# Groups of one batch, and a unit without attention that computes v on GpSimd, in a fused attention and two-MoE kernel

## The chip, the cores and the metric

The kernel runs on one core of one Trainium2 chip. The metric is the device time of one execution in microseconds (us); lower is better. The engines that matter are PE (TensorE, matrix multiplies), DVE (VectorE), ACT (ScalarE), POOL (GpSimd) and the DMA engines, which are fed from the queues of SP (SyncE) and POOL.

## What is computed

```python
# attention, batch by batch: 8 batches, 3072 tokens, 256 wide, keys of 64
scores = z @ z.T / 3072
out    = (relu(scores) ** 2) @ v
x      = u * out                                    # 24576 tokens x 256

# first MoE: a token with x @ w_skip > 0 goes to one of 8 experts (256 -> 1024 -> 256)
e      = argmax(x @ w_gate)
x[tok] += gate[tok] * (relu(x[tok] @ w1[e]) @ w2[e])

# second MoE: one dense rational layer (256 -> 2048 -> 256)
h = x @ w_in
P = a0 + a1*h + a2*h**2 + a3*h**3
Q = 1 + |b0|*|h| + |b1|*h**2
out = (P / (Q + 1e-6)) @ w_out
```

All of it is float32. Every large product is made of three passes of a split operand (high and low part), which is why there are pairs of tiles such as ah and al, mgh and mgl.

## The kernel before

**Work items.** Attention is cut into 1152 ticks (8 batches, 12 rows of 256 queries, 12 steps of 256 keys). A tick is 16 matmuls of 256 columns on PE (4 for the scores, L661 and L662; 12 for the product with v, L684), two or three ACT passes (L665, L668, L409) and one DVE subtraction (L676). After every 12 ticks a row of queries is routed: a chain of small steps over PE, ACT, DVE and POOL ends in indirect writes of the rows to a DRAM buffer xs, sorted by expert.

The MoE work is cut into 1024 units of 24 (or 18) matmuls on PE. 256 of them belong to the first MoE (kinds "m" and "n": ReLU on ACT, L1249, and one subtraction on DVE, L1252). 768 belong to the second (kinds "x" and "y"). A second-MoE unit evaluates the rational layer on a 128x512 tile h in PSUM:

- ACT: abs, u = |h| (L1257); p1 (L1258); ln (L1272) and ex (L1273), which turn the denominator q into its reciprocal u.
- q0 = b1\*u + b0 (POOL or DVE L1264, or ACT L1262) and q1 = q0\*u (L405, POOL or DVE).
- DVE: p2 (L1270), p3 (L1271), gh (L1274, the high part of the result, tile mgh), v = (q + c)\*gh (L1275), w (L1277), and gl (L405, POOL or DVE, the low part, tile mgl).

gh and gl feed the second product (L1095). h sits in one of five PSUM banks of ring "b" from the first matmul of the unit until w.

**Groups.** The batches are cut into groups of 1, 2, 2, 2 and 1. A group's attention is done, its rows are sorted by expert, its first-MoE units run (8 experts, 4 chunks of weights, and as many halves as the group has batches), and then its second-MoE units. In a group of two batches one chunk of first-MoE weights (tile W, 1 MB, loaded at L993 from the copy wsc1) serves two units, with matmuls of 512 columns (mm_l1w, L1077); in a group of one it serves one unit with matmuls of 256 columns (mm_l1, L1066). Attention ticks of the following groups are mixed among the units: kind "x" is a second-MoE unit that runs beside ticks, kind "y" one that runs after the last tick. The last group's first-MoE units are kind "n"; they use the attention's V buffers for weights (tile Wv) and run among "y" units. Between the last tick and the last group lie 56 "y" units of the group before (number POST) and the 32 "n" units; we call this stretch the bridge.

**Order.** The program's order is not that of the loops. Each step is given a due time (a place of its unit or tick on a line of PE time, plus an offset from LAG, plus a correction from the table PAR). The class Flow then lays the steps on the engines one by one with costs such as "D.602" (0.602 us on DVE) and ring sizes from RINGS, and each engine runs its own list in that order. W has a ring of 8 buffers, mu and mq of 3, mp of 2, mr (rows of a tile) of 4. SP's queue is in order too: a W load that waits for a free buffer holds up what stands behind it.

## Time and profile before

| | us |
|---|---|
| median of 3 runs | 5582.74 (5581.83 to 5587.68) |
| the profiled execution | 5577.05 |
| its span (first to last instruction) | 5575.3 |

| stretch of the profiled execution, us | length | what runs in it (counts from the loops) |
|---|---|---|
| 0 to 366 | 366 | attention alone, 168 ticks |
| 366 to 511 | 145 | group 0, first MoE: 32 m, and 12 ticks |
| 511 to 1301 | 790 | group 0, second MoE: 80 x with 276 ticks |
| 1301 to 1520 | 219 | group 1, first MoE: 64 m with 12 ticks |
| 1520 to 2663 | 1143 | group 1, second MoE: 192 x with 288 ticks |
| 2663 to 2882 | 219 | group 2, first MoE: 64 m with 12 ticks |
| 2882 to 3980 | 1098 | group 2, second MoE: 192 x with 264 ticks |
| 3980 to 4200 | 220 | group 3, first MoE: 64 m with 12 ticks |
| 4200 to 4895 | 695 | group 3, second MoE: 152 x with 108 ticks |
| 4895 to 5192 | 297 | bridge: 56 y and 32 n |
| 5192 to 5575 | 383 | group 4, second MoE: 96 y |

The limits of the stretches are the first ACT steps of their kind in the trace (abs of the second MoE, ReLU of the first), so the last steps of a unit spill over into the next stretch. Busy time of PE is modelled and counts overlapped matmuls; what PE does not fill is idle for certain, what it fills may still hold short waits.

### The profile page before, as it was taken

What the parts mean: (1) busy time and instruction counts of PE and PEld (TensorE: products, weight loads), DVE (VectorE), ACT (ScalarE), POOL (GpSimd) and SP (SyncE); (2) the same over time, 40 slices, a digit from 0 to 9 for tenths busy, and PEclk for the clock granted to TensorE, in tenths of its full rate; (3) what the DMA queues carried; (4) which work ended last, traced back from release to release, by engine and by line L of the source; (5) the groups of instructions that cost most, each with busy time, mean ns of one, the idle gap of its engine ahead of it and who ended that gap; (6) DMA issues with size and microseconds to landing.
All of it is one profiled execution on the core that took longest, in us unless ns stands there. A gap on an engine that the chain in (4) does not pass through costs nothing.

```text
span 5575.3 us, 107018 instructions
## 1 busy us (share of the span) xinstructions
PE 5362.4 (96%) x39525; PEld 5027.9 (90%) x39525; DVE 4533.8 (81%) x7470; ACT 4202.2 (75%) x7663; POOL 3090.5 (55%) x4422
## 2 busy tenths in 40 slices
PE   9989999999999999999999999999999999999887
PEld 8989999999899999999899989999988888888666
DVE  6765777774498999899459999999638999998998
ACT  8866888885388888888448888888627888855776
POOL 3433445443256655665235566556526667765887
PEclk9999999999999999999999999999999999999999
DMA  4375111114510110112541010011351000044000
GB/s 136 115 273 218 64 51 42 34 53 176 176 60 32 45 40 31 31 41 76 178 154 36 32 50 27 29 32 48 132 207 63 24 25 20 25 157 140 16 16 17
DMA packets 205545, 435.31 MB, mean 78 GB/s; under 512 B 30094, under 2 KB 129017, under 8 KB 181458
## 3 DMA queue, kind: packets, MB, share of 16 engines
q1 hardware_dynamic: 177746, 360.66, 19.1%
q0 software_dynamic: 27264, 67.71, 3.5%
q8 instruction: 313, 5.13, 0.4%
q14 instruction: 222, 1.82, 0.1%
HBM read 308.56 MB, written 153.22 MB: 83 GB/s over the span
## 4 chain that ended last, share of the span: by engine, by line
PE 70%; DVE 13%; ACT 6%; DMA 4%; issue 4%; POOL 3%; SPq 0%; DVEq 0%; ACTq 0%; POOLq 0%
PE accA L684 24%; PE h L1077 17%; PE accM L1095 16%; PE S L661 4%; PE S L662 4%; DVE mq L1275 3%; DVE mgh L1274 3%; DMA mr<-xs 2%; DVE h L1271 2%; DVE mq L1277 2%; DVE mp L1270 1%; PE lp L773 1%; PE mt L1130 1%; ACT mp L1258 1%; ACT mu L1272 1%
## 5 line engine op out<-in xcount | busy, mean ns | idle before, releaser
L1077 PE MATMUL h<-mx,W 128*128 128x512 f32 x5760 | 1540.7, 400 | 64.1 <-DVE mq L1277 58.9
L684 PE MATMUL accA<-V,ah 128*128 128x256 f32 x9216 | 1270.0, 280 | 13.1 <-ACT ah L409 8.3
L405 POOL TENSOR_TENSOR mgl<-mq,mu 128x512 fp32r<-128x512 f32 x655 | 892.1, 1363 | 692.9 <-DVE mq L1277 395.8
L1077 PEld LDWEIGHTS h<-mx,W 128*128 128x128 f32 x5760 | 1013.5, 190 | 250.6 <-DVE mq L1277 75.3
L684 PEld LDWEIGHTS accA<-V,ah 128*128 128x128 f32 x9216 | 1164.4, 189 | 31.5 <-ACT ah L409 14.5
L1095 PE MATMUL accM<-W,mgh 128*128 128x256 f32 x7680 | 1054.5, 280 | 10.6 <-DVE mgh L1274 6.6
L1095 PEld LDWEIGHTS accM<-W,mgh 128*128 128x128 f32 x7680 | 979.6, 189 | 32.3 <-DVE mgh L1274 8.9
L676 DVE TENSOR_TENSOR al<-S,ah 128x512 fp32r<-128x512 f32 x1152 | 786.3, 683 | 168.4 <-ACT ah L409 143.9
L665 ACT ACTIVATE S<-S 128x512 f32<-128x512 f32 x1152 | 677.9, 588 | 119.2 <-PE S L662 109.5
L684 PE MATMUL accA<-V,al 128*128 128x256 f32 x4608 | 729.7, 281 | 5.9 <-DVE al L676 5.7
L1264 POOL TENSOR_SCALAR mq<-mu,coef 128x512 f32<-128x512 f32 x554 | 458.0, 827 | 473.1 <-ACT mu L1257 467.6
L668 ACT ACTIVATE S<-S 128x512 f32<-128x512 f32 x1152 | 676.0, 587 | 21.8
L1270 DVE TENSOR_TENSOR mp<-mp,h 128x512 f32<-128x512 f32 x768 | 522.3, 680 | 187.0 <-ACT mp L1258 178.1
L1257 ACT ACTIVATE mu<-h 128x512 f32<-128x512 f32 x768 | 458.0, 596 | 271.0 <-PE h L1077 212.2
L409 ACT ACTIVATE ah<-S 128x512 fp32r<-128x512 f32 x996 | 594.9, 598 | 63.3 <-PE accA L684 41.7
L1095 PE MATMUL accM<-W,mgl 128*128 128x256 f32 x3840 | 615.1, 282 | 27.9 <-POOL mgl L405 27.3
L1274 DVE SCALAR_TENSOR_TENSOR mgh<-h,coef,mu 128x512 fp32r<-128x512 f32 x768 | 571.3, 744 | 80.2 <-ACT mu L1273 64.9
L684 PEld LDWEIGHTS accA<-V,al 128*128 128x128 f32 x4608 | 621.4, 189 | 13.5 <-DVE al L676 8.2
L1275 DVE SCALAR_TENSOR_TENSOR mq<-mq,mgh 128x512 f32<-128x512 f32 x768 | 617.4, 805 | 15.7 <-DVE mgh L1274 0.5
L1272 ACT ACTIVATE mu<-mq 128x512 f32<-128x512 f32 x768 | 483.3, 629 | 179.1 <-POOL mq L405 138.6
L1258 ACT ACTIVATE mp<-h,coef 128x512 f32<-128x512 f32 x768 | 595.5, 775 | 23.3 <-DVE h L1271 18.8
L1095 PEld LDWEIGHTS accM<-W,mgl 128*128 128x128 f32 x3840 | 537.3, 189 | 63.4 <-POOL mgl L405 39.7
(157 smaller groups left out, 8466.9 us busy)
## 6 DMA issues: line engine op xcount, KB each, us to landing
W<-wsc SPq DMA_DIRECT2D x96, 1024.0 KB
wsc<-W SPq DMA_DIRECT2D x32, 1024.0 KB
...
```

Of the source, the lines that this page charges most:

```text
L405: (nc.vector if e == "D" else nc.gpsimd).tensor_tensor(*a, **k)
L409: act(out, in_, AF.Copy)
L665: act(st["s"], st["s"], AF.Relu, scale=1.0 / S)
L668: act(st["s"], st["s"], AF.Square)
L676: ttt(st["lo"], st["s"], st["hi"].bitcast(F32), op=ALU.subtract)
L684: mm(accs[b, ic][:, it * TT : (it + 1) * TT], lhsT=a[:, jj * TT + it * P : jj * TT + (it + 1) * P], rhs=VV[b, jp][:, vi, jj * D : (jj + 1) ...
L1077: mm(h, lhsT=lw, rhs=rw, start=(k == 0 and i == 0), stop=(k == NK - 1 and i == 2), skip_group_check=True)
L1095: mm(accs_[it // 2][:, it % 2 * TT : (it % 2 + 1) * TT], lhsT=(gh, gl)[part][:, it * P : (it + 1) * P], rhs=w[i][:, 512 + ff * D : 512 + ( ...
L1258: pt("p1", "A.664", ["l1b"], lambda: act(buf("mp"), s["h"], AF.Identity, scale=a3, bias=a2), ["mp"])
L1270: pt("p2", "D.602", ["p1", "abs"], lambda: ttt(s["p"], s["p"], s["h"], op=ALU.mult))
L1274: pt("gh", "D.663", ["ex", "p3"], lambda: stt(buf("mgh", F32R), s["h"], a0, s["u"], op0=ALU.add, op1=ALU.mult), ["mgh"])
L1275: pt("v", "D.602s", ["gh"], lambda: stt(s["q"], s["q"], CQ, s["gh"].bitcast(F32), op0=ALU.add, op1=ALU.mult))
```

## The change

Three things change in the source, and with them the order of nearly all instructions:

- GROUPS becomes eight groups of one batch. All 256 first-MoE units now use one chunk of weights each, with matmuls of 256 columns. POST goes from 56 to 40 and MROW from 8 to 16 (12 ticks are spread over the first 16 units of a first-MoE stretch).
- "y" units compute differently. A new ACT step qc (L1281) adds the constant to q. v becomes a plain product on POOL (L1285) in place of the DVE step L1275. w writes into h (L1286), and gl (L1287) is always on DVE and reads h. q1 is always on POOL. mu uses the attention's T1 buffers (6) and mq the wr buffers (4) in place of 3 and 3. h is held until gl, not w. In the last group every sixth unit takes its h from the accumulator bank accA.
- The tables PAR, SLIP, AHEAD, LAG of "y" and the planned PE costs get new numbers, and two 64-byte spacers (ahead of T4 and V) are gone.

| after: stretch | what runs in it (counts from the loops) |
|---|---|
| attention alone; group 0, first MoE | 168 ticks; 32 m and 12 ticks |
| group 0, second MoE | 80 x with 132 ticks |
| groups 1 to 6, first MoE, each | 32 m with 12 ticks |
| groups 1, 2, 3, second MoE, each | 96 x with 144 ticks |
| groups 4, 5, second MoE, each | 96 x with 132 ticks |
| group 6, second MoE | 72 x with 72 ticks |
| bridge | 40 y and 32 n |
| group 7, second MoE | 96 y |

```diff
-GROUPS = [1, 2, 2, 2, 1]
+GROUPS = [1, 1, 1, 1, 1, 1, 1, 1]
...
-SLIP = {"P": 8.95, "A": 0.25, "D": 24.11, "G": 5.02, "Q": 9.0}
-LEAD, TAIL, POST, CARRY, MROW = 24, 8, 56, 1, 8
-PE_TICK, PE_UNIT = 1.92, 2.87
+SLIP = {"P": 8.1, "A": 0.25, "D": 32.01, "G": 33.99, "Q": 9.0}
+LEAD, TAIL, POST, CARRY, MROW = 24, 8, 40, 1, 16
+PE_TICK, PE_UNIT = 1.87, 2.8
...
+        home = {"mgh": ghb, "mgl": glb}
+        if kd == "y":
+            home.update(mu="T1", mq="wr")
...
-        hu = ("b", ("u", t))
+        hb = "accA" if kd == "y" and m.g == NG - 1 and (t - len(munits)) % 6 == 0 else "b"
+        hu = (hb, ("u", t))
...
-            pt("q1", "D.602s|G1.245t", ["q0"], lambda e: tt_on(e, s["q"], s["q"], s["u"], op=ALU.mult))
+            pt("q1", "G1.245t" if kd == "y" else "D.602s|G1.245t", ["q0"], lambda e="G": tt_on(e, s["q"], s["q"], s["u"], op=ALU.mult))
...
+            if kd == "y":
+
+                pt("qc", "A.52", ["q1"], lambda: act(s["q"], s["q"], AF.Identity, bias=CQ))
+                pt("ln", "A.52", ["qc"], lambda: act(s["u"], s["q"], AF.Ln))
+                pt("ex", "A.52", ["ln"], lambda: act(s["u"], s["u"], AF.Exp, scale=-1.0))
+                pt("gh", "D.663", ["ex", "p3"], lambda: stt(buf("mgh", F32R), s["h"], a0, s["u"], op0=ALU.add, op1=ALU.mult), ["mgh"])
+                pt("v", "G1.245t", ["gh"], lambda: pool_tt(s["q"], s["q"], s["gh"].bitcast(F32), op=ALU.mult))
+                pt("w", "D.663", ["v"], lambda: stt(s["h"], s["h"], a0, s["q"], op0=ALU.add, op1=ALU.subtract), (), ["mq"])
+                pt("gl", "D.602", ["w"], lambda: ttt(buf("mgl", F32R), s["h"], s["u"], op=ALU.mult), ["mgl"], ["mu"], [hu])
```

The order moves in these places. In the names, the number after h, mp, mq, mu, mgh and mgl is the unit; the last group of the kernel holds units 928 to 1023. DVE in the middle of the last group, before:

```order
L1270 TENSOR_TENSOR mp994_72646<-mp994_72646,h994_72582 128x512
L1277 SCALAR_TENSOR_TENSOR mq993_72629<-h993_72535,coef_103,mq993_72629 128x512
L1271 SCALAR_TENSOR_TENSOR h994_72582<-mp994_72646,coef_103,h994_72582 128x512
L1274 SCALAR_TENSOR_TENSOR mgh994_72720<-h994_72582,coef_103,mu994_72667 128x512
L1270 TENSOR_TENSOR mp995_72683<-mp995_72683,h995_72596 128x512
L1275 SCALAR_TENSOR_TENSOR mq994_72677<-mq994_72677,mgh994_72720 128x512
```

and after:

```order
L1286 SCALAR_TENSOR_TENSOR h994_74135<-h994_74135,coef_109,mq994_74195 128x512
L1278 SCALAR_TENSOR_TENSOR h996_74212<-mp996_74285,coef_109,h996_74212 128x512
L1287 TENSOR_TENSOR mgl994_74341<-h994_74135,mu994_74179 128x512
L1286 SCALAR_TENSOR_TENSOR h995_74174<-h995_74174,coef_109,mq995_74238 128x512
L1284 SCALAR_TENSOR_TENSOR mgh996_74361<-h996_74212,coef_109,mu996_74264 128x512
L1287 TENSOR_TENSOR mgl995_74364<-h995_74174,mu995_74216 128x512
L1277 TENSOR_TENSOR mp997_74314<-mp997_74314,h997_74231 128x512
```

DVE has five steps a unit in both. L1275 (v), which read the two SBUF tiles mq and mgh, is gone, and gl (L1287), which reads h, has come. POOL at the same place, before:

```order
L1264 TENSOR_SCALAR mq994_72677<-mu994_72667,coef_103 128x512
L405 TENSOR_TENSOR mq994_72677<-mq994_72677,mu994_72667 128x512
L405 TENSOR_TENSOR mgl992_72703<-mq992_72616,mu992_72602 128x512
L405 TENSOR_TENSOR mgl993_72712<-mq993_72629,mu993_72618 128x512
L1264 TENSOR_SCALAR mq995_72728<-mu995_72718,coef_103 128x512
```

and after:

```order
L1271 TENSOR_SCALAR mq996_74287<-mu996_74264,coef_109 128x512
L405 TENSOR_TENSOR mq996_74287<-mq996_74287,mu996_74264 128x512
L1285 TENSOR_TENSOR mq994_74195<-mq994_74195,mgh994_74298 128x512
L1285 TENSOR_TENSOR mq995_74238<-mq995_74238,mgh995_74308 128x512
L405 TENSOR_TENSOR mq997_74328<-mq997_74328,mu997_74296 128x512
L1271 TENSOR_SCALAR mq998_74351<-mu998_74338,coef_109 128x512
```

POOL's v (L1285) stands where its gl (L405 into mgl) stood. In the last 96 units POOL has 70 q0, 96 q1 and 96 gl before, and 73 q0, 96 q1 and 96 v after; ACT has 26 q0 before, and 23 q0 and 96 qc after. SP's queue in a first-MoE stretch of group 1 before (W is a chunk of weights, mr the rows of a tile):

```order
L1119 DMA mr17_0_20491<-xs1_73 128x516
L993 DMA W61_20525<-wsc1_70 128x2048
L1119 DMA mr17_1_20569<-xs1_73 128x516
L993 DMA W62_20583<-wsc1_70 128x2048
L993 DMA W63_20629<-wsc1_70 128x2048
L993 DMA W64_20705<-wsc1_70 128x2048
L1119 DMA mr18_0_20723<-xs1_73 128x516
```

and of group 2 after:

```order
L1119 DMA mr32_0_25131<-xs2_75 128x516
L993 DMA W98_25173<-wsc1_70 128x2048
L993 DMA W99_25224<-wsc1_70 128x2048
L993 DMA W100_25257<-wsc1_70 128x2048
L993 DMA W101_25308<-wsc1_70 128x2048
L763 DMA x2_3_78<-xs39_24278 128x2x256
L1119 DMA mr33_0_25337<-xs2_75 128x516
```

Four W loads lie between the rows of two tiles in both, but before they serve eight units, after four.

## Rows read from the trace of the kernel before

**Rows 1.** The page, busy time and share of PE and its span.
```profile
span 5575.3 us, 107018 instructions
...
PE 5362.4 (96%) x39525; PEld 5027.9 (90%) x39525; DVE 4533.8 (81%) x7470; ACT 4202.2 (75%) x7663; POOL 3090.5 (55%) x4422
```

**Rows 2.** Windows by stretch: limits, length, each engine's busy us (instructions), clock, DMA.
```profile
366.00:511.00 145.00, 128.06 (x1038) 125.03 (x1037) 76.98 (x133) 74.21 (x135) 39.73 (x73) 0.98 0.86 321
511.00:1301.00 790.00, 785.87 (x6266) 761.22 (x6264) 601.35 (x1049) 667.48 (x1287) 375.25 (x743) 1.00 0.17 55
1301.00:1520.00 219.00, 212.82 (x1448) 194.24 (x1447) 78.55 (x139) 70.20 (x127) 50.12 (x98) 1.00 0.54 191
1520.00:2663.00 1143.00, 1134.85 (x8549) 1074.10 (x8548) 1045.83 (x1736) 976.70 (x1792) 683.93 (x1000) 1.00 0.14 44
2882.00:3980.00 1098.00, 1086.97 (x8136) 1030.44 (x8135) 1018.66 (x1684) 945.78 (x1723) 672.35 (x940) 1.00 0.13 43
...
4200.00:4895.00 695.00, 662.40 (x4609) 608.10 (x4608) 669.88 (x1053) 574.27 (x1012) 502.10 (x553) 0.99 0.10 32
4895.00:5192.00 297.00, 274.08 (x1890) 249.61 (x1889) 265.80 (x384) 174.54 (x290) 186.59 (x190) 0.98 0.39 131
5192.00:5575.00 383.00, 301.79 (x1778) 250.77 (x1778) 359.79 (x500) 271.40 (x433) 325.11 (x265) 0.97 0.05 18
```

**Rows 3.** The same, abs alone (L1257): its count is the units' count.
```profile
1520.00:2663.00 1143.00, 114.53 (x192) 1.00 0.14 44
...
4200.00:4895.00 695.00, 90.65 (x152) 0.99 0.10 32
4895.00:5192.00 297.00, 33.45 (x56) 0.98 0.39 131
5192.00:5575.00 383.00, 56.98 (x96) 0.97 0.05 18
```

**Rows 4.** The same, the first ReLU of a tick alone (L665).
```profile
511.00:1301.00 790.00, 161.74 (x276) 1.00 0.17 55
...
4200.00:4895.00 695.00, 62.25 (x106) 0.99 0.10 32
```

**Rows 5.** DVE groups, 5200 to 5500: line, tiles, count | busy us, mean ns | idle before.
```profile
L1275 DVE SCALAR_TENSOR_TENSOR mq<-mq,mgh 128x512 f32<-128x512 f32 x78 | 80.3, 1029 | 3.2
L1277 DVE SCALAR_TENSOR_TENSOR mq<-h,coef,mq 128x512 f32<-128x512 f32 x79 | 58.4, 740 | 0.0
L1274 DVE SCALAR_TENSOR_TENSOR mgh<-h,coef,mu 128x512 fp32r<-128x512 f32 x78 | 58.3, 748 | 5.2 <-ACT mu L1273 1.0
L1271 DVE SCALAR_TENSOR_TENSOR h<-mp,coef,h 128x512 f32<-128x512 f32 x78 | 58.1, 745 | 0.7
L1270 DVE TENSOR_TENSOR mp<-mp,h 128x512 f32<-128x512 f32 x78 | 52.6, 675 | 1.3 <-ACT mp L1258 1.3
L1139 DVE TENSOR_TENSOR mx<-mt,mx 128x512 fp32r<-128x512 f32 x10 | 6.8, 682 | 0.0
```

**Rows 6.** DVE groups, 2000 to 2600: v beside attention.
```profile
L1275 DVE SCALAR_TENSOR_TENSOR mq<-mq,mgh 128x512 f32<-128x512 f32 x101 | 76.2, 754 | 1.7
```

**Rows 7.** POOL and ACT groups, 5200 to 5500.
```profile
L405 POOL TENSOR_TENSOR mgl<-mq,mu 128x512 fp32r<-128x512 f32 x79 | 114.7, 1452 | 6.3 <-DVE mq L1277 6.3
L405 POOL TENSOR_TENSOR mq<-mq,mu 128x512 f32<-128x512 f32 x78 | 106.1, 1370 | 4.1
...
L1272 ACT ACTIVATE mu<-mq 128x512 f32<-128x512 f32 x78 | 48.8, 626 | 43.2 <-POOL mq L405 43.2
L1264 POOL TENSOR_SCALAR mq<-mu,coef 128x512 f32<-128x512 f32 x59 | 47.4, 803 | 26.7 <-ACT mu L1257 26.7
```

**Rows 8.** Waits, 5200 to 5500: who for whom, us in total, times, longest.
```profile
PE h L1077 <- DVE mq L1277: 35.2, 45, 2.1
```

**Rows 9.** First-MoE matmuls of the last group (L1066): duration, first and last start.
```profile
L1066 PE MATMUL h<-mx,Wv x384: 274/283/387, 4931.8 to 5127.7; 128*128 128x256 f32 x192
```

**Rows 10.** PE group of the tile transposes, 1380 to 1520.
```profile
L1130 PE MATMUL mt<-ident_r,mr 128*128 128x128 f32 x48 | 7.5, 279 | 5.5 <-DMA mr<-xs 5.5
```

**Rows 11.** DMA, 1280 to 1540, in 40 slices: rate in GB/s.
```profile
GB/s 61 3 21 64 358 418 43 275 81 161 40 185 222 220 224 166 205 225 174 219 284 200 265 208 202 193 196 223 216 183 255 98 255 5 197 150 9 0 184 147
```

More of the change, by code (lines that the diff above doesn't have):

```diff
@@ L696, in plan_tick @@
             sf.append(("T1", ("T1", b, jp // 2)))
-        add(at["S"], ("S", n), "P.476", scores, after=sd, takes=[("b", ("S", n))], frees=sf)
+        add(at["S"], ("S", n), "P.467", scores, after=sd, takes=[("b", ("S", n))], frees=sf)
         add(at["relu"], ("relu", n), "A.478", relu, after=[("S", n)])
@@ L1234, in buf, with pt @@
         def buf(tag, dt=F32):
-            o = s[tag[1:]] = tl({"mgh": ghb, "mgl": glb}.get(tag, tag), f"{tag}{t}", dt)
+            o = s[tag[1:]] = tl(home.get(tag, tag), f"{tag}{t}", dt)
             return o
-        def pt(n, ops, after, fn, takes=(), frees=()):
+        def pt(n, ops, after, fn, takes=(), frees=(), more=()):
             add(
                 at[n], (n, t), ops, fn, after=[(a, t) for a in after],
-                takes=[(r, ("u", t)) for r in takes], frees=[(r, ("u", t)) for r in frees],
+                takes=[(home.get(r, r), ("u", t)) for r in takes],
+                frees=[(home.get(r, r), ("u", t)) for r in frees] + list(more),
             )
         prev = [("l1a", t - 1)] if t else []
-        pl1 = "P.714" if m.nh == 1 else "P.69"
+        pl1 = "P.7" if m.nh == 1 else "P.696"
         add(at["l1a"], ("l1a", t), pl1, lambda: l1(0), after=prev + [("m", m.mi, h, "lo") for h in range(m.nh)] + [("W", wn)], takes=[hu])
@@ L1281, in plan_unit @@
         add(
-            at["l2h"], ("l2h", t), "P.952", lambda: l2(0), after=[("gh", t)] + ([("l2l", m.ts[fp - 1])] if fp else []),
+            at["l2h"], ("l2h", t), "P.932", lambda: l2(0), after=[("gh", t)] + ([("l2l", m.ts[fp - 1])] if fp else []),
             takes=[(acc_tag(m), ("m", m.mi, h)) for h in range(m.nh)] if first else [],
```

52 lines of the change are left out of this document (25 added, 27 removed), and 39 rows, old and new, of tables (LAG, PAR).

## Prediction

> **What bounds the kernel now.** I read the page first: PE is busy 96% of the span [rows 1], so PE is the engine to watch, and the question is where it is not paced by its own work. The windows by stretch answer that [rows 2]. From 511 to 3980 us PE is busy 97 to 99.5%: in the stretches where units and ticks run together (1143 us and 1098 us) nothing else is full; DVE is at 91 to 93%. Three late stretches differ. From 4200 to 4895 DVE is at 96% and PE at 95%. In the bridge PE has 23 us idle, in the last group 81 us of 383. There DVE is at 94%, POOL at 85%, ACT at 71%: DVE sets the pace.
>
> Prices of PE-paced work come from two stretches: 790 us for 80 x and 276 ticks, 1143 us for 192 x and 288 ticks [rows 2 to 4]. They give 2.0 us a tick and 2.95 a unit; the stretch with 264 ticks (1098 us) pulls that to 1.97 and 3.0, which I use: 784, 1143 and 1096 us. A first-MoE unit costs (219 - 12 x 1.97) / 64 = 3.05 us in groups of two, and (145 - 24) / 32 = 3.79 in group 0, whose units have a weight chunk each, as all have after the change, but also prepare it.
>
> By these prices the late stretches lose: 695 - (152 x 3.0 + 108 x 1.97) = 26 us; 297 - 88 x 3.0 = 33 us; 383 - 96 x 3.0 = 95 us. Together 154 us. This is what the change can win back.
>
> Why the last group is slow: 78 units pass in 300 us, 3.82 us each. DVE's five steps take 675, 745, 748, 740 and, for v, 1029 ns [rows 5]. Beside attention the same v takes 754 [rows 6]. v alone of the five reads two SBUF tiles, the others read h in PSUM, and POOL is busy with two-tile products of its own [rows 7]. I read this as v waiting for POOL's products. PE in turn waits 35 us for w, which frees a bank for the next h [rows 8].
>
> **The change, part by part.**
>
> *Units without attention (y).* DVE loses v (1029 ns) and gains gl, a product with h in PSUM like p2 (675 ns); w keeps its form. DVE's busy time per unit was 360 / 96 = 3.75 us; it becomes 3.75 - 0.35 = 3.40. POOL's was 325 / 96 = 3.39; it trades gl (1452 ns) for v, which the trace doesn't show on POOL: bounds are q1's 1370 and gl's 1452, both the same kind of product, so 3.3 to 3.4. ACT's was 271 / 96 = 2.83; qc adds one pass like ln, 626 ns [rows 7], so 3.45 at most; it can no longer rest. Three engines then lie between 3.3 and 3.5, PE at 3.0. DVE kept 96% of the pace before (3.75 of 3.82, with its drain); 3.40 / 0.97 is 3.5 us. The bounds are 3.25 (DVE's steps overlap a little more once v's waits are gone) and 3.82 (nothing won). The extra holding time of h (v on POOL is 0.6 us longer, qc 0.6, gl 0.7) would be felt through the banks; the sixth bank from accA and the deeper mu and mq rings are the cover. Without it, PE's wait for h would grow again and y would stay near 3.8.
>
> The last group then takes 96 x 3.5, and at its end the 16 us that the last units need to drain, plus 1.5 for qc and the slower v: 353.5 in place of 383, **-29.5 us**.
>
> *Bridge.* The first n matmul starts at 4931.8, 37 us after the stretch begins [rows 9]: the last rows' routing must end first, so fewer or faster y units don't shorten it. Then came 32 y and 32 n in 198 us (3.1 each), then 16 y in 62 us. After the change 16 y and 32 n stand in the middle: DVE has room, so 48 x 3.1 = 149 us; then 16 x 3.5 = 56. 37 + 149 + 56 = 242 in place of 297, of which 16 units (48 us) have moved into mixed stretches: **-7 us** (0 to -20).
>
> *Mixed stretches.* The even ones keep their price, so cutting them into groups of one costs and gives nothing by itself: 1.38 to 1.65 ticks a unit are PE-paced before as well. What is won is the thin one. From its windows DVE needs 3.47 us per x and 1.32 per tick. At 0.71 ticks a unit that is 4.41 against PE's 4.40, hence the 26 us lost; at 1.0 it is 4.79 against 4.97. So 72 x with 72 ticks lose between nothing and 0.17 us a unit; I take 7 us in total: **-19 us**.
>
> *First MoE in groups of one.* 192 units change from 6 matmuls of 512 columns to 12 of 256, the same columns. Each unit now needs a chunk of its own: 1 MB, and a quarter of the tile's rows in and out (2 x 64 KB), 1.18 MB per unit in place of 0.66. SP's queue has one W load per unit, and mr loads behind them; the mr ring of 4 now reaches over four tiles, not two, so the transposes' waits for rows (5.5 us in 140 [rows 10]) should shrink. The best case is PE without its idle 6 us in 219: 0.1 us a unit, -19 us. Against it stands the feed. Group 0 moved 321 GB/s at a DMA share of 0.86 [rows 2], some 373 if full (an estimate from that row); single slices of 6.5 us show 418 [rows 11]. At 373 a unit is fed in 3.16 us. In the 16 units of a stretch that have ticks beside them PE needs over 4 us, so the eight W buffers fill up; the other 16 (96 in all) would lack 0.11 each, partly covered by the buffers. I take **+5 us**, with -19 and +142 (all 192 at group 0's 3.79) as ends.
>
> The page "DMA: Bandwidth & Descriptors" of the Trainium skill (section "Where 436 GB/s comes from") speaks against this part: it puts what one core gets from HBM at about 358 GB/s. By that a unit would be fed in 3.30 us, and the sum below would be some 20 us smaller. The slices at 418 GB/s do not agree with it as a ceiling.
>
> *Smaller edits.* The planner's new numbers change the order within stretches that are PE-paced; I cost that at nothing, with the work of PE as the cover, and keep 10 us either way. Routing, prefill and the number of batch changes stay.
>
> **Sum.** -29.5 - 7 - 19 + 5 = -50.5 us on the profiled execution's 5577.05, so 5526.5. The median of the runs shown is 5.7 us above it: 5532.
>
> **The rivals.**
>
> A. *The bound moves to POOL and ACT.* v on POOL stands in line behind q0 and q1 of later units, qc makes ACT nearly full, and DVE's w waits for POOL's v. y stays at 3.82; the last group gains nothing and loses 1.5, the bridge gains 2. For it: three engines within 5%, five banks and a longer chain. Against it: in the order q1 of a unit and its v lie two to three units apart, some 8 us, and ACT's three steps and gh between them need about 3. Sum: +1.5 - 2 - 19 + 5 = -14.5, so 5568.
>
> The Trainium skill's page "Perfetto Trace Analysis" (section "Optimizing Scalar/DVE Operations") warns that work moved between DVE and GpSimd may not help, since the two share a read port. By that warning A would be what happens. The trace agrees with the sharing in v's 1029 against 754 ns, but shows no such lengthening in the steps that read h, and those are all that DVE keeps.
>
> B. *The weights come too late.* One chunk per unit starves the first-MoE stretches, PE waits at L1066, and all 192 units cost what group 0's cost: +142 in place of +5, 5532 + 137 = 5669, slower. It decides the sign from 3.05 + 55 / 192 = 3.34 us a unit on, that is if less than about 353 GB/s arrive. For it: 0.86 DMA share in group 0. Against it: ACT and DVE prepared weights there, and DMA's stores ran beside the loads. Half of it (only the units without ticks) gives 5532 + 66 = 5598.
>
> C. *Everything is covered.* y at 3.25, no PE idle in the first MoE, no loss in the thin mixture: -24 - 4 - 24 - 7, so 5473.
>
> D. *The even rate does not do what it says*: the loss of the thin stretch turns up at 1.0 ticks as well, and six boundaries in place of three cost 3 to 5 us each. Then 5532 + 19 + 10 = 5561.
>
> **Chances.** Forecast 0.50; A 0.16; B 0.13 (half of it as the milder form); C 0.11; D 0.10. The predicted time is the forecast's, 5532. The range reaches from C (5473) to B's milder form (5598): **5475 to 5595**. About 0.2% (11 us) is what a measurement of this kernel can tell from no change, so "same" is 5571.6 to 5593.9. Faster takes the forecast, C, D and most of A: 0.79. Same takes the rest of A and some of B: 0.09. Slower is most of B: 0.12.
>
> **What would show it.** In the profile after: the last group's units at 3.5 us each, no DVE step over 0.76 us there, v on POOL at 1.3 to 1.5 us, POOL and DVE both above 90%. First-MoE stretches of about 122 us with 32 units and 12 ticks; waits of PE at L1066 for a W load would mean B. The stretch with one tick a unit at about 365 us. Wrong would be: DVE waiting for POOL's v in most units (A), or stretches of 135 us and more in the first MoE (B).

## The result, and the profile after

The changed kernel takes **5502.59 us** (median of 4 runs, 5501.92 to 5506.9) beside 5583.42 us before (5581.83 to 5587.68): 81 us less, a ratio of 0.9856, 95% interval 0.9839 to 0.9873. The forecast was 5532 in a range of 5475 to 5595. Direction and range held; the gain was 81 us where 50.5 was the sum. The profiled execution has a span of 5500.2 us, 75.1 less than before.

The windows of the changed kernel by stretch, with the columns of [rows 2]: group 0's first and second MoE, group 1's first and second, the second MoE of groups 2, 4 and 6, the bridge and the last group.

```profile
367.00:518.00 151.00, 134.32 (x1055) 131.19 (x1055) 82.08 (x142) 78.74 (x142) 40.66 (x74) 0.94 0.90 343
518.00:1021.00 503.00, 497.09 (x3764) 472.14 (x3763) 453.69 (x748) 429.43 (x795) 300.41 (x455) 1.00 0.19 63
1021.00:1143.00 122.00, 121.59 (x1037) 121.16 (x1036) 44.52 (x82) 47.96 (x90) 32.79 (x73) 1.00 0.78 283
1143.00:1718.00 575.00, 568.50 (x4275) 539.12 (x4274) 525.71 (x855) 492.00 (x897) 344.66 (x498) 1.00 0.18 57
1838.00:2415.00 577.00, 569.58 (x4271) 539.30 (x4270) 528.83 (x862) 487.47 (x888) 345.99 (x500) 1.00 0.18 59
3233.00:3787.00 554.00, 544.74 (x4067) 515.15 (x4066) 522.01 (x852) 465.84 (x850) 327.93 (x461) 1.00 0.18 58
4581.00:4931.00 350.00, 346.26 (x2516) 324.27 (x2514) 337.07 (x536) 294.99 (x526) 256.37 (x304) 1.00 0.13 42
4931.00:5162.00 231.00, 214.64 (x1552) 198.87 (x1552) 173.14 (x270) 150.39 (x256) 151.33 (x162) 1.00 0.50 165
5162.00:5500.00 338.00, 290.96 (x1812) 250.73 (x1810) 321.15 (x507) 302.30 (x533) 303.05 (x269) 0.98 0.06 20
```

The first MoE of group 1 has PE busy for 121.59 of 122 us: the weights are not late. The last group takes 338 us in place of 383, and its DVE, ACT and POOL are busy for 95, 89 and 90% of it, the drain at the end included.

The engines in the middle of the last group (5183 to 5463), columns as in [rows 5], the answer to [rows 5 and 7]: first DVE, then POOL, then ACT.

```profile
L1286 DVE SCALAR_TENSOR_TENSOR h<-h,coef,mq 128x512 f32<-128x512 f32 x85 | 63.7, 750 | 0.4 <-POOL mq L1285 0.3
L1278 DVE SCALAR_TENSOR_TENSOR h<-mp,coef,h 128x512 f32<-128x512 f32 x85 | 63.1, 746 | 0.5
L1284 DVE SCALAR_TENSOR_TENSOR mgh<-h,coef,mu 128x512 fp32r<-128x512 f32 x85 | 63.0, 742 | 1.6 <-ACT mu L1283 0.9 <-PE accM L1095 0.6
L1287 DVE TENSOR_TENSOR mgl<-h,mu 128x512 fp32r<-128x512 f32 x84 | 57.1, 679 | 0.1
L1277 DVE TENSOR_TENSOR mp<-mp,h 128x512 f32<-128x512 f32 x85 | 56.2, 676 | 0.7 <-ACT mp L1265 0.7
...
L405 POOL TENSOR_TENSOR mq<-mq,mu 128x512 f32<-128x512 f32 x86 | 111.2, 1297 | 5.9 <-ACT mq L1269 1.9 <-DVE h L1278 0.5
L1285 POOL TENSOR_TENSOR mq<-mq,mgh 128x512 f32<-128x512 f32 x85 | 109.7, 1297 | 5.1 <-DVE mgh L1284 5.1
L1271 POOL TENSOR_SCALAR mq<-mu,coef 128x512 f32<-128x512 f32 x65 | 50.4, 776 | 5.1 <-ACT mu L1264 4.6 <-POOL mq L1285 0.2
...
L1281 ACT ACTIVATE mq<-mq 128x512 f32<-128x512 f32 x85 | 53.6, 631 | 7.0 <-POOL mq L405 6.5
```

85 units in 280 us are 3.29 us each, where [rows 5] gave 3.82. DVE hardly ever waits (the last column sums to 3.3 us) and no step has a mean over 750 ns. POOL's two products take 1297 ns each; before they took 1370 and 1452 [rows 7]. Of the wait that stood at 35.2 us in 300 us in [rows 8], 12.6 in 280 us are left (second line):

```profile
PE accM L1095 <- DVE mgl L1287: 13.2, 21, 1.3
PE h L1077 <- DVE mgl L1287: 12.6, 11, 2.8
```

**Where the 75 us came from.** By the prices of the prediction (1.97 us a tick, 3.0 a second-MoE unit, 3.05 a first-MoE unit) all the kernels' work costs 5354.2 us, whatever the groups. What a stretch takes beyond its price is its loss; a negative loss means that the work was cheaper there than its price. The table has the losses, in us, of each profiled execution; a stretch begins with the first ACT step of its first unit, and each group's first MoE is counted together with its second, since work slides over that limit. "Even" are the groups between group 0 and the last with ticks; "late" is that last one with its ticks (0.71 a unit with the old groups, 1.0 with groups of one).

| kernel | attention alone, group 0 | even | late | bridge | last group | sum |
|---|---|---|---|---|---|---|
| before | 67.7 | 1.7 | 25.6 | 30.9 | 95.0 | 220.9 |
| new y, old groups, old tables (e5) | 69.4 | 3.2 | 22.0 | 27.6 | 51.9 | 174.1 |
| new y, groups of one, old tables (e9) | 69.4 | 16.6 | 8.9 | 19.8 | 50.8 | 165.5 |
| changed kernel (new tables) | 72.0 | 22.4 | -11.8 | 13.8 | 49.6 | 146.0 |
| old y, groups of one, old tables (e6) | 71.2 | 14.0 | 8.6 | 43.3 | 121.0 | 258.1 |
| old y, groups of one, new tables (e2) | 70.8 | 27.2 | -12.3 | 52.5 | 119.0 | 257.2 |
| new y, old groups, new tables (e1) | 110.5 | 20.0 | 25.7 | 28.6 | 48.8 | 233.6 |

The first four rows are the change in three steps: the new unit gives 47 us, the groups 9, the tables 19 (by the medians below 50, 14 and 18). The order of the steps matters: without the new unit the groups cost 31 us (e6), and the new tables on the old groups cost 53 (e1).

### The profile page after: what moved, and what is told of

Read it like the earlier page. It is cut to its first block, busy times and chain, and to the rows that moved or that the text cites. A ratio compares the mean times of both kernels' runs of the same rounds, so it can differ in the third digit from the quotient of the medians.

```text
span 5500.2 us, 109355 instructions
## 1 busy us (share of the span) xinstructions
PE 5350.1 (97%) x40680; PEld 5091.0 (93%) x40680; DVE 4516.0 (82%) x7487; ACT 4247.7 (77%) x7757; POOL 3094.2 (56%) x4485
## 4 chain that ended last, share of the span: by engine, by line
PE 74%; DVE 12%; ACT 4%; DMA 3%; POOL 3%; issue 3%; SPq 0%; POOLq 0%; DVEq 0%; ACTq 0%
PE accA L684 24%; PE h L1077 14%; PE accM L1095 14%; PE accM L1085 5%; PE h L1066 5%; PE S L661 4%; PE S L662 4%; DVE mp L1277 2%; DVE h L1278 1%; DVE mq L1292 1%; PE lp L773 1%; DVE mgh L1291 1%; PE mt L1130 1%; DVE al L676 1%; DMA wr<-in_moe_w_dram 1%
## 5 line engine op out<-in xcount | busy, mean ns | idle before, releaser
L1077 PE MATMUL h<-mx,W 128*128 128x512 f32 x4608 | 1212.6, 398 | 30.6 <-DVE mgl L1287 21.1
L405 POOL TENSOR_TENSOR mgl<-mq,mu 128x512 fp32r<-128x512 f32 x494 | 661.3, 1339 | 715.0 <-DVE mq L1294 412.0
L1077 PEld LDWEIGHTS h<-mx,W 128*128 128x128 f32 x4608 | 810.2, 188 | 176.1 <-DVE mgl L1287 25.6
L665 ACT ACTIVATE S<-S 128x512 f32<-128x512 f32 x1152 | 678.9, 589 | 238.8 <-PE S L662 227.0
L1095 PE MATMUL accM<-W,mgh 128*128 128x256 f32 x6144 | 844.3, 280 | 13.0 <-DVE mgh L1291 10.7
L1095 PEld LDWEIGHTS accM<-W,mgh 128*128 128x128 f32 x6144 | 777.3, 189 | 22.3 <-DVE mgh L1291 12.6
L684 PEld LDWEIGHTS accA<-V,al 128*128 128x128 f32 x4608 | 628.0, 189 | 19.8 <-DVE al L676 11.7
L409 ACT ACTIVATE ah<-S 128x512 fp32r<-128x512 f32 x956 | 570.8, 597 | 76.1 <-PE accA L684 40.8
L662 PE MATMUL S<-T,T 128*128 128x256 f32 x2304 | 594.7, 282 | 0.0
L1278 DVE SCALAR_TENSOR_TENSOR h<-mp,coef,h 128x512 f32<-128x512 f32 x768 | 573.2, 747 | 4.7
L405 POOL TENSOR_TENSOR mq<-mq,mu 128x512 f32<-128x512 f32 x393 | 521.0, 1327 | 39.5 <-ACT mq L1269 14.0
L1095 PE MATMUL accM<-W,mgl 128*128 128x256 f32 x3072 | 491.7, 282 | 26.2 <-DVE mgl L1287 22.3
L661 PE MATMUL S<-T,T 128*128 128x256 f32 x1920 | 505.8, 287 | 4.8 <-DVE mq L1294 2.3
```

The lines of the kernel that those rows point to most:

```text
L405: (nc.vector if e == "D" else nc.gpsimd).tensor_tensor(*a, **k)
L661: mm(o, lhsT=lw, rhs=rw, start=(jj == 0), stop=False, skip_group_check=True)
L662: mm(o, lhsT=lw, rhs=T4[b, ic], start=False, stop=(jj == 1), skip_group_check=True)
L665: act(st["s"], st["s"], AF.Relu, scale=1.0 / S)
L684: mm(accs[b, ic][:, it * TT : (it + 1) * TT], lhsT=a[:, jj * TT + it * P : jj * TT + (it + 1) * P], rhs=VV[b, jp][:, vi, jj * D : (jj + 1) ...
L1077: mm(h, lhsT=lw, rhs=rw, start=(k == 0 and i == 0), stop=(k == NK - 1 and i == 2), skip_group_check=True)
```

## The experiments

Times are medians; "the kernel before" ran on the same chip each time and took 5584.5 to 5584.6.

### The two halves alone (e1, e2)

The new unit with the groups of before:

```diff
-GROUPS = [1, 1, 1, 1, 1, 1, 1, 1]
+GROUPS = [1, 2, 2, 2, 1]
...
-LEAD, TAIL, POST, CARRY, MROW = 24, 8, 40, 1, 16
+LEAD, TAIL, POST, CARRY, MROW = 24, 8, 56, 1, 8
```

> The changed kernel with the groups of before (1, 2, 2, 2, 1, with POST 56 and MROW 8 as there): the new unit without attention alone, with the new tables. Theory S (the two parts add, and the new unit is the larger): the last group keeps the 338 us that it takes in the changed kernel, in place of 383 (-45), the bridge's 40 y in front of or behind its n units lose up to 0.5 us each (-10 to -20), the thin stretch of 0.71 ticks a unit stays at about 695 us. Together -50 to -60 us: 5525 to 5535. Rival G (most of it comes from the groups, whose tables only fit them): under -30 us, over 5553, with the last group above 355 us.

Measured 5588.38 us, ratio 1.0005 (0.9995 to 1.0014): nothing gained. The last group is at 336.8 us, as in the changed kernel, so the unit does there what it should. The 46 us were lost again in the mixed stretches: group 0's second MoE 824 us where it was 792, groups of two 12 to 26 us longer in the second MoE (8 to 13 shorter in the first), the late group 708 where it was 695. None of them holds a unit of the new kind. Either the tables or the unit itself had to be the cause.

Groups of one with the old unit:

```diff
-            home.update(mu="T1", mq="wr")
...
-        hb = "accA" if kd == "y" and m.g == NG - 1 and (t - len(munits)) % 6 == 0 else "b"
+        hb = "b"
...
-            pt("q1", "G1.245t" if kd == "y" else "D.602s|G1.245t", ["q0"], lambda e="G": tt_on(e, s["q"], s["q"], s["u"], op=ALU.mult))
+            pt("q1", "D.602s|G1.245t", ["q0"], lambda e="G": tt_on(e, s["q"], s["q"], s["u"], op=ALU.mult))
...
-            if kd == "y":
...
-            else:
+            if True:
```

(What follows is the old branch: v on DVE, w into q, gl on POOL or DVE. LAG and the corrections of y are the old ones, all other tables the new.)

> The changed kernel with the unit without attention written as before (v on DVE, gl on POOL, three mu, three mq, no sixth bank): groups of one alone. Theory S: the last group stays at about 383 us (y at 3.8), the stretch with one tick a unit takes 350 us and so loses nothing, 16 fewer y units save 13 us, the first-MoE stretches take 120 to 122 us as in the changed kernel, the even stretches 575 and 554. Together -25 us, 5550 to 5565, and with the first run the two differences add up to some -81. Rival G: under 5535, with a last group under 360 us.

Measured 5610.34 us, ratio 1.0044 (1.0027 to 1.0061): slower, where 25 us of gain were expected. Mixed stretches and first MoE are those of the changed kernel to within 4 us, as expected. But the last group takes 407 us, not 383, and the bridge 270. DVE in its last group (5225 to 5505):

```profile
L1251 DVE SCALAR_TENSOR_TENSOR mq<-mq,mgh 128x512 f32<-128x512 f32 x69 | 62.3, 903 | 0.7
...
L375 DVE TENSOR_TENSOR mq<-mq,mu 128x512 f32<-128x512 f32 x22 | 20.3, 923 | 0.0
L375 DVE TENSOR_TENSOR mgl<-mq,mu 128x512 fp32r<-128x512 f32 x14 | 10.8, 770 | 0.0
```

In these 280 us 36 of the two-tile products q1 and gl stand on DVE, the engine that is full; in [rows 7] all are on POOL. The planner may choose ("D.602s|G1.245t"); it counts 0.602 us for such a product on DVE, and in this stretch they take 770 to 923 ns.

### Tables apart from the change (e5, e6, e9)

The three kernels start from the kernel before, with its tables. The first has the new unit (and the new LAG and corrections of y), the second the groups, the third both.

```diff
-LEAD, TAIL, POST, CARRY, MROW = 24, 8, 56, 1, 8
+LEAD, TAIL, POST, CARRY, MROW = 24, 8, 40, 1, 16
...
-GROUPS = [1, 2, 2, 2, 1]
+GROUPS = [1, 1, 1, 1, 1, 1, 1, 1]
...
-    spacers = {"T4": 16, "V": 16, "ah": 16, "W": 16, "mgh": 16, "mx": 16}
+    spacers = {"ah": 16, "W": 16, "mgh": 16, "mx": 16}
```

> The kernel before with the new unit without attention, the groups and the tables of before (only LAG and the corrections of y are the new ones): what the first run did, without its new tables. Theory T (the two halves add, but the tables belong to their mixtures: in the first run the mixed stretches of the old groups lost some 100 us by the new tables, while the last group took 336.8 as in the changed kernel): the mixed stretches keep the lengths of before to within 3 us each, the last group takes 337 (-46), the bridge up to 10 less. 5525 to 5540. Rival I (the old groups suffer from the new unit itself, by its rings or its places): mixed stretches as in the first run, 5570 or more.

Measured 5534.92 us, ratio 0.9918 (0.9902 to 0.9935). Theory T holds: the mixed stretches are those of before to within 2.5 us, the last group takes 340. The unit alone is worth 50 us, and the new tables on the old groups cost 53 (5588.4 less 5534.9).

> The kernel before with groups of one batch (POST 40, MROW 16), its old unit without attention and its old tables (and without the two spacers of 64 bytes, which no longer fit): what the second run did, without its new tables. Theory T: the last group takes 380 to 385 us and the bridge 240 to 250, where the second run's 407 and 270 came from the new tables, by which old units got some q1 and gl on DVE; the mixed stretches are up to 10 us longer each than in the changed kernel, since the old tables belong to 3.45, 1.5, 1.38 and 0.71 ticks a unit: 5550 to 5590. Rival U (the tables do nothing for the mixture, so the mixed stretches are as in the changed kernel): 5540 to 5555. Rival V (the tables carry the whole gain of the mixture): mixed stretches 15 us longer each and more, over 5620.

Measured 5615.31 us, ratio 1.0058 (1.0041 to 1.0075). Of the mixed stretches the late one is 14 us longer than in the changed kernel, where T allowed 10; the others are at most 1 us longer and up to 8 shorter, so neither U nor V holds. The last group does not fit T at all: 409 us, with 27 q1 and 11 gl on DVE in 280 us. So it isn't the new tables that spoil the old unit; with groups of one the planner gives DVE these products under either set of tables. My reason in the expectation was wrong. In the changed kernel the engine of q1, v and gl is fixed, and in the seven kernels with the unit unchanged the last group takes 336.6 to 339.9 us, whatever groups and tables they have.

> Groups of one and the new unit without attention together, with the tables of before (and without the two spacers): the changed kernel less its new tables. Theory A (stage by stage the parts add): up to the bridge as in the sixth run, 11 us above the changed kernel, all of it in the stretch with one tick a unit; bridge 231 to 235; last group 340 as in the fifth run. Some 5513 to 5520, 10 to 15 us above the changed kernel. Rival B (the parts only work together with tables made for them, as the first, second and sixth run seemed to say): over 5535.

Measured 5520.54 us, ratio 0.9887 (0.9871 to 0.9904): 18 us above the changed kernel, where theory A said 10 to 15, and just over its range. Stage by stage A holds: the losses up to the bridge are those of e6 to within 3 us, that of the last group is e5's to within about 1 us; the bridge takes 237 us where A said 231 to 235. The tables are a third part of the gain, not a condition of the others. They act mainly in the late group, which with its first MoE gains 20.7 us by them (the bridge gains 6, the even groups lose 6): its second MoE, 72 x with 72 ticks, takes 365 us under the old tables and 350 under the new. DVE there, old tables first (4578 to 4943), then the changed kernel (4581 to 4931):

```profile
L1262 DVE SCALAR_TENSOR_TENSOR mq<-mq,mgh 128x512 f32<-128x512 f32 x71 | 68.2, 962 | 0.6
...
L375 DVE TENSOR_TENSOR mq<-mq,mu 128x512 f32<-128x512 f32 x37 | 28.3, 764 | 0.1
```

```profile
L1292 DVE SCALAR_TENSOR_TENSOR mq<-mq,mgh 128x512 f32<-128x512 f32 x70 | 58.7, 838 | 1.2
...
L405 DVE TENSOR_TENSOR mq<-mq,mu 128x512 f32<-128x512 f32 x27 | 20.8, 772 | 1.2 <-POOL mq L1271 1.0
```

Ten q1 fewer on DVE, and a v of 838 ns in place of 962: 17 us of DVE's time, about the 15 that the stretch is shorter (DVE's busy time as a whole falls by 12.6, from 349.65 to 337.07).

### What made v slow (e3, e7, e11)

Only the rings and the sixth bank, in the kernel before:

```diff
+        home = {"mgh": ghb, "mgl": glb}
+        if kd == "y":
+            home.update(mu="T1", mq="wr")
...
+        hb = "accA" if kd == "y" and m.g == NG - 1 and (t - len(munits)) % 6 == 0 else "b"
```

> The kernel before with only the longer rings and the sixth bank for the unit without attention (mu in the six T1 buffers, mq in the four wr buffers, every sixth h of the last group in accA); v stays on DVE, gl on POOL, no qc. Theory W (y is slow since v reads two SBUF tiles and waits for POOL's products, so that DVE is full): v stays near 1 us, y near 3.8, the last group near 380 us, the time within 8 us of before. Rival R (y is slow since PE waits for a bank and POOL for a buffer; DVE's steps are long only by chance): y falls to 3.3 to 3.5, the last group to 330 to 355, the time by 30 to 55 us.

Measured 5592.53 us, ratio 1.0016 (1.0006 to 1.0026): theory W. The last group takes 392 us, and v 934 ns (66.5 us for 72, 5209 to 5489). The longer rings bring nothing while DVE is full. (The planner also put 12 q1 and 8 gl on DVE in these 280 us, so it is not the old unit to the letter.)

The unit of the changed kernel with v on DVE and gl on POOL:

```diff
-                pt("v", "G1.245t", ["gh"], lambda: pool_tt(s["q"], s["q"], s["gh"].bitcast(F32), op=ALU.mult))
-                pt("w", "D.663", ["v"], lambda: stt(s["h"], s["h"], a0, s["q"], op0=ALU.add, op1=ALU.subtract), (), ["mq"])
-                pt("gl", "D.602", ["w"], lambda: ttt(buf("mgl", F32R), s["h"], s["u"], op=ALU.mult), ["mgl"], ["mu"], [hu])
+                pt("v", "D.602s", ["gh"], lambda: ttt(s["q"], s["q"], s["gh"].bitcast(F32), op=ALU.mult))
+                pt("w", "D.663", ["v"], lambda: stt(s["q"], s["h"], a0, s["q"], op0=ALU.add, op1=ALU.subtract), (), ())
+                pt("gl", "G1.245t", ["w"], lambda: pool_tt(buf("mgl", F32R), s["q"], s["u"], op=ALU.mult), ["mgl"], ["mu", "mq"], [hu])
```

> The changed kernel with v on DVE and gl on POOL in the unit without attention, and w into q; qc, the longer rings, the sixth bank and q1 on POOL stay. As many steps on each engine as in the changed kernel. Theory W (v is the only one of DVE's steps that reads two SBUF tiles, and it waits for POOL's products): v takes 0.9 to 1.05 us, POOL's products 1.35 to 1.45 in place of 1.30, y 3.65 to 3.85 and the last group 370 to 385 us. Rival N (which engine has v doesn't matter, q1 fixed on POOL and the rings did it): v at 0.75, y 3.3 to 3.4, the last group 338 to 348 us.

Measured 5565.33 us, ratio 0.9971 (0.9956 to 0.9986), 63 us above the changed kernel; the last group takes 383 us, as before the change. Theory W, in its numbers (5195 to 5475):

```profile
L1285 DVE TENSOR_TENSOR mq<-mq,mgh 128x512 f32<-128x512 f32 x74 | 74.4, 1024 | 0.6
...
L405 POOL TENSOR_TENSOR mq<-mq,mu 128x512 f32<-128x512 f32 x73 | 101.4, 1391 | 12.7 <-ACT mq L1269 10.2
L1287 POOL TENSOR_TENSOR mgl<-mq,mu 128x512 fp32r<-128x512 f32 x75 | 99.1, 1331 | 29.9 <-DVE mq L1286 28.4 <-ACT mp L1265 1.5
```

DVE has five steps a unit and POOL two products, as in the changed kernel; only which product stands where differs. POOL even has less to do: 37 q0 stand on it here and 65 in the changed kernel's 280 us (ACT does the rest), and it is busy for 233.5 us in place of 263.9. Still v is back at 1024 ns, and the units at 3.78 us.

v and gl both on DVE:

```diff
-                pt("v", "G1.245t", ["gh"], lambda: pool_tt(s["q"], s["q"], s["gh"].bitcast(F32), op=ALU.mult))
+                pt("v", "D.602s", ["gh"], lambda: ttt(s["q"], s["q"], s["gh"].bitcast(F32), op=ALU.mult))
```

> The changed kernel with v on DVE and gl left there: DVE has six steps a unit without attention, POOL only q0 and q1. Theory W (v's length follows how much of the time POOL spends on products of two tiles: 754 ns at a share of 0.27, 900 at 0.52, 934 at 0.62, 1025 at 0.72 to 0.73 in the traces so far): with one product of 1.3 us a unit the share is 0.32 and v takes 750 to 820 ns; y is 3.25 + 0.75 = 4.0 us, the last group 405 to 415, the time 65 to 80 us above the changed kernel. Rival X (v is long in any stretch without attention): v at 0.95 to 1.05, y 4.2 to 4.3, the last group 430 or more.

Measured 5583.22 us, ratio 0.9996 (0.9986 to 1.0006). With one product a unit left on POOL, v takes 728 ns beside the same units without attention (5189 to 5469), even less than theory W's 750 to 820, so the stretch as such is not what makes it slow. The last group takes 413 us, for DVE has six steps:

```profile
L1285 DVE TENSOR_TENSOR mq<-mq,mgh 128x512 f32<-128x512 f32 x68 | 48.5, 728 | 0.0
```

The single instructions show how it comes about. DVE and POOL in the kernel before, from 5301 on (start, duration in us, engine):

```profile
5301.54 1.28 POOL L405 TENSOR_TENSOR mq<-mq,mu 128x512 f32<-128x512 f32 x1
5301.74 1.63 DVE L1275 SCALAR_TENSOR_TENSOR mq<-mq,mgh 128x512 f32<-128x512 f32 x1
...
5302.78 1.77 POOL L405 TENSOR_TENSOR mgl<-mq,mu 128x512 fp32r<-128x512 f32 x1
```

v begins 0.2 us after POOL's product and ends 0.55 us behind its end; POOL's next product begins while v is open and takes 1.77 us instead of 1.3. Sorted over the last groups of the kernels with v on DVE, by what was open when a step began (worked out from starts and ends of all v and all two-tile products on POOL; "alone" is without such a product, means in ns unless it says median):

| kernel | v begins beside an open POOL product | v ends after that product's end, median | v begins alone | POOL product begins beside an open v | POOL product begins alone |
|---|---|---|---|---|---|
| before | 66, 1172 ns | 550 ns | 31, 715 ns | 56, 1685 ns | 138, 1300 ns |
| e3 | 36, 1307 | 548 | 64, 696 | 43, 1656 | 128, 1314 |
| e7 | 52, 1264 | 550 | 46, 797 | 29, 1651 | 168, 1304 |
| e11 | 9, 1019 | 549 | 91, 682 | 6, 1740 | 90, 1291 |

Whichever of the two begins first has its own length, the other stands until it ends; a POOL product that begins beside an open v ends 1147 to 1169 ns after v's end (10th to 90th percentile of the kernel before). Some v that begin without a product beside them are longer too (up to 1.2 us in e7). These begin beside an open q0, the POOL step that reads one SBUF tile, as in e7:

```profile
5231.59 0.78 POOL L1271 TENSOR_SCALAR mq<-mu,coef 128x512 f32<-128x512 f32 x1
...
5231.78 1.12 DVE L1285 TENSOR_TENSOR mq<-mq,mgh 128x512 f32<-128x512 f32 x1
```

v ends 0.54 us after q0's end. The v that begin with nothing open on POOL (47 in e3, 24 in e7, 86 in e11) take 670 to 694 ns, none longer; in the kernel before every v begins beside a product or a q0. q0 waits in turn: the five that begin beside an open v in the kernel before have a mean of 1149 ns, the others 771. So the partner is not the product alone. The mean share of POOL's products does not tell v's length by itself: in the late group under the old tables v takes 962 ns at a share of 0.37 (87.1 and 46.1 us of products in 365), and in the last group of e3 934 at 0.62. What counts is what begins beside what.

The Trainium skill's page "SBUF — State Buffer" (section "Who interferes with whom") states this rule: a DVE instruction with two SBUF inputs contends with a GpSimd instruction that reads SBUF, one with at most one does not (outside its two-port modes), and the order of issue decides who blocks. The traces agree with all three: 1.63 us in the timeline against some 0.69 alone for v, 676 to 750 ns for the steps that read h in PSUM beside the same products, and both orders in the table.

### The cover (e8)

The new unit with three mu, three mq and five banks:

```diff
-            home.update(mu="T1", mq="wr")
+            home.update()
...
-        hb = "accA" if kd == "y" and m.g == NG - 1 and (t - len(munits)) % 6 == 0 else "b"
+        hb = "b"
```

> The changed kernel with three mu and three mq buffers and five banks, as before, in the unit without attention. Theory C (the longer chain needs the cover): units wait for mq and mu and PE for banks, y 3.6 to 3.9, the last group 365 to 395 us. Rival F (DVE sets the pace, and five banks are enough): y up to 3.35, the last group 338 to 345 us. Theory C's condition from the trace of the changed kernel: from its first matmul to gl a unit holds h for some 12 us, 3.6 units of 3.285, so three mq buffers held from q0 to w would just do and three mu from abs to gl not.

Measured 5577.94 us, ratio 0.9993 (0.9982 to 1.0003), 75 us above the changed kernel: theory C, and somewhat more than it said. The last group takes 401 us, more than with the old unit. DVE, now with idle time, then PE's wait (5192 to 5472):

```profile
L1277 DVE TENSOR_TENSOR mp<-mp,h 128x512 f32<-128x512 f32 x70 | 47.9, 685 | 39.1 <-ACT mu L1264 34.8 <-ACT mp L1265 4.3
```

```profile
PE h L1077 <- DVE mgl L1287: 48.5, 39, 2.5
```

So neither half of the unit does anything alone (the rings, and the split that puts v on POOL and gl on DVE): rings without the split 392 us, the split without rings 401, both but with v on DVE 383, all together 338. How much of e8 is due to the banks and how much to mu and mq was not taken apart.

### Even rate or fewer groups (e4, e10)

Batches grouped 1, 2, 2, 1, 1, 1, in the changed kernel and in e9:

```diff
-GROUPS = [1, 1, 1, 1, 1, 1, 1, 1]
+GROUPS = [1, 2, 2, 1, 1, 1]
```

> The changed kernel with batches grouped 1, 2, 2, 1, 1, 1: two boundaries between groups fewer, with the mixture still at 0.83 ticks a unit or more. Theory N (a boundary between groups costs something of its own: in the changed kernel PE idles 15 to 18 us in each second-MoE stretch of 96 units where it idled 20 to 25 in one of 192, while the first MoE in groups of one loses 2 us in place of 4 per 32 units): two boundaries fewer save some 3 to 5 us each, 6 to 10 us under the changed kernel, about 5495. Rival E (the even rate is what matters, each step down in the rate costs): 0 to 20 us above the changed kernel, since the rates are 1.44, 1.12, 1.0 and 0.83.

> The run before, with batches grouped 1, 2, 2, 1, 1, 1: the question of the fourth run again, without the new tables, which there cost the mixture of 3.45 ticks a unit 32 us. Theory N (a boundary between groups costs 3 to 5 us of its own): two boundaries fewer bring 6 to 10 us under the run before. Rival E (the even rate is what matters): the stretches at 1.0 and 0.83 ticks a unit lose 6 and 12 us more, so 5 to 15 us above it. If neither is larger than 5 us, cutting into groups costs nothing and gives only the late stretch its ticks.

Measured 5597.31 us (ratio 1.0022, 1.0012 to 1.0032) and 5575.84 us (0.9986, 0.9977 to 0.9996): 95 and 55 us above the kernels that they come from. The direction is rival E's, and both are far beyond what either theory allowed. In e10 the losses by the prices are 78.8 up to group 0 (e9: 69.4), 55.5 in the three groups after it (16.6) and 17.6 in the late one (8.9). The worst is the group of 96 x with 96 ticks, 33 us with its first MoE, at the same rate of 1.0 at which e9's 72 units lost 9. DVE is busy for 480 of its 508 us, and v takes 898 ns (4019 to 4527):

```profile
L1262 DVE SCALAR_TENSOR_TENSOR mq<-mq,mgh 128x512 f32<-128x512 f32 x95 | 85.3, 898 | 1.1
...
L375 DVE TENSOR_TENSOR mq<-mq,mu 128x512 f32<-128x512 f32 x51 | 39.9, 783 | 3.3 <-POOL mq L1241 3.2
```

Fewer boundaries are worth nothing that can be seen beside this loss. That the lower rates make it is not shown: attention alone and group 0, with the same 3.45 ticks a unit as in e5, lose 9 us more than there, and the group at 1.44 ticks loses 13.5 where e5's at 1.5 lost 1.0. Why the same rate costs four times as much in a longer stretch stays open; the number of products on DVE per unit is alike (0.53 and 0.51 q1).

### How near the feed is (e12)

Each reloaded chunk of first-MoE weights loaded twice:

```diff
-                nc.sync.dma_start(out=wt_t["tile", n].bitcast(F32), in_=wsc1[c].bitcast(F32))
+                for _ in range(2):
+                    nc.sync.dma_start(out=wt_t["tile", n].bitcast(F32), in_=wsc1[c].bitcast(F32))
```

> The changed kernel with each first-MoE chunk from the second group on loaded twice into the same tile: 2.2 MB per unit in place of 1.2. It measures how much the feed can give. Theory F (the feed is near its limit in the changed kernel: 283 GB/s at a DMA share of 0.78 are 363 if full): 2.2 MB take 6 us, and less the eight chunks that are loaded ahead a first-MoE stretch takes 150 to 190 us in place of 120; six of them and the bridge add 200 to 450 us. Rival M (there is room for twice as much, since the loads spread into the stretch ahead): stretches up to 130 us, at most 60 us in all.

Measured 6160.45 us, ratio 1.1035 (1.1013 to 1.1057). Every first-MoE stretch takes 222 to 229 us in place of 117 to 119 (from its first ReLU to the first abs). Window and PE's longest waits of group 1's (1029 to 1252):

```profile
1029.00:1252.00 223.00, 139.00 (x1005) 135.90 (x1005) 44.04 (x80) 46.67 (x87) 31.27 (x68) 0.78 0.74 279
```

```profile
PE mt L1131 <- DMA mr<-xs: 36.1, 3, 14.2
PE h L1067 <- DMA W<-wsc: 28.5, 8, 6.3
```

Theory F in direction, and dearer than it said. The rate is 279 GB/s at a DMA share of 0.74, about what the changed kernel has in its stretch (283 at 0.78): the bytes grew 1.8 times (34.5 to 62.1 MB) and so did the time. It is no clean measure of the limit: group 0's first MoE moves 343 GB/s at a share of 0.90 in the changed kernel, the second load of a tile goes into the buffer of the first and probably waits for it (not shown), and PE's clock was granted at 0.78, which makes part of the 101 us between the two windows. The doubled bytes in the 122 us of the changed kernel would be 509 GB/s, more than any slice of it shows (430). So the changed kernel has less than twice the feed that it needs; how much it has this run does not show. The longest single wait is for the rows mr, which stand behind the weights on SP's queue.

## Why the prediction was right, and by what it was off

- **Last group, forecast -29.5, measured -45.4.** The mechanism was right: v did wait for POOL's products. In its new place it takes 1.297 us, under its bounds of 1.370 and 1.452, since no v on DVE makes POOL's products wait any more. The step that was mis-sized is y, 3.5 us where 3.29 was measured: I took DVE's busy time per unit, 3.75 over the whole group, down by 0.35 us (v less gl) and its share as 97%. (The 96% beside it is wrong: 3.75 of 3.82 is 98%.) In the middle 280 us of the group, after and then before, the windows say:

```profile
5183.00:5463.00 280.00, 252.06 (x1570) 216.45 (x1570) 276.77 (x434) 263.55 (x465) 263.93 (x236) 1.00 0.05 18
```

```profile
5212.00:5492.00 280.00, 229.86 (x1346) 191.05 (x1346) 270.18 (x375) 203.58 (x326) 246.22 (x201) 0.98 0.05 16
```

  That is 270.18 / 73.3 = 3.69 us of DVE a unit before (280 / 3.82 units, busy 96%), and 276.77 / 85 = 3.26 after (busy 99%): 0.43 less: 0.35 for v less gl, and 0.08 since the steps that remain overlap a little more (their mean lengths, with the mx steps, sum to 4.02 us a unit before and 3.67 after). The other way round, the drain was too cheap: from the last abs to the end it takes 25.5 us, and 19.7 before. Counted as in the sum, 96 units of 3.285 make 315 of the 338 us and leave 22, where I had put 17.5.
- **Bridge, -7 against -17.1** (297 - 48 = 249 to 231). The matmuls of the first n unit show the parts: 4970.2 to 5112.1 us, so 39 us ahead (forecast 37), 142 for 48 units (149), 50 for the 16 y behind (56). The new unit alone gives 3 of it (e5); the rest came with groups and tables.

```profile
L1066 PE MATMUL h<-mx,Wv x384: 274/283/285, 4970.2 to 5112.1; 128*128 128x256 f32 x192
```

- **Thin stretch, -19 against -37** (25.6 to -11.8 with its first MoE). Half of it is the rate (8.9 in e9), half the tables (-20.7). I had costed the tables at nothing, plus or minus 10; on the whole kernel they are 18 us, and with other groups 53 the wrong way. That step was wrong: the work of PE did not cover the order. In the late stretch the order acts through v, whose length depends on what POOL does beside it (962 to 838 ns), and through the q1 on DVE. The 53 us on the old groups have another cause, which stays open: in group 0, 32 us longer in e1, v takes what it took (511 to 1303 before, 522 to 1346 in e1), while PE is busy for 805.91 of 824 us there and for 787.87 of 792 before.

```profile
L1275 DVE SCALAR_TENSOR_TENSOR mq<-mq,mgh 128x512 f32<-128x512 f32 x80 | 55.2, 690 | 1.9
```

```profile
L1292 DVE SCALAR_TENSOR_TENSOR mq<-mq,mgh 128x512 f32<-128x512 f32 x80 | 55.2, 691 | 2.4
```

- **Even mixed stretches, 0 against +20.7.** "Cutting them into groups of one costs and gives nothing" was wrong: each group of one loses 3.7 to 5.5 us (0.7 to 5.7 in e9) where a group of two lost 0.4 to 1.3. That was rival D's price per boundary (3 to 5), and I gave it only to the case in which the late stretch lost too.
- **First MoE, +5 against about -10** (the stretches ahead of the bridge taken alone, with losses of 15.1 us before and 5.1 after; part of it is work that slid into the stretch behind, so it is in the table above with the second MoE). PE waits there for no weights; the stretches are 117 to 119 us from first step to first step, 122 was said to be the sign. Rival B did not come: single slices (3.05 us each) of group 1's stretch (1021 to 1143) move up to 430 GB/s, beside the mean of 283:

```profile
GB/s 124 0 11 325 361 348 78 306 430 277 225 377 307 199 368 325 212 264 295 199 390 280 348 165 309 352 372 367 362 411 425 363 408 349 260 406 344 85 290 0
```

  The term that was mis-sized is the full rate, 321 / 0.86 = 373 GB/s. The kernel before has a stretch in group 0's first MoE (387 to 437) in which the DMA engines are busy for 90% or more in every slice (the digit 9), and it moves more:

```profile
DMA  9999999999999999999999999999999999999999
...
DMA packets 8761, 19.90 MB, mean 398 GB/s; under 512 B 756, under 2 KB 6828, under 8 KB 7226
```

  At 398 a unit's 1.18 MB would take 2.96 us (an estimate, from other traffic than that of the later groups), less than PE's 3.05, and nothing would be lacking.

- Together the mixed part with its first MoE was forecast at -14 and measured at -12.4 (+20.7 - 37.4, and +4.3 up to group 0): right only because its errors cancel. The 25 us by which the span beat the sum are the last group (16) and the bridge (10).
- **Rival A** (the bound moves to POOL and ACT) failed on its own condition: DVE's w waited 0.3 us for POOL's v in 280 us. The warning of the Trainium skill's page "Perfetto Trace Analysis" (section "Optimizing Scalar/DVE Operations"), that moving work between DVE and GpSimd may not help, would have been right for a swap that leaves a two-tile product on DVE: e7 is that case, 383 us. Here all that DVE kept reads h in PSUM.
